# An FNet mixing and squared-ReLU FFN kernel: GpSimd's products get a second operation, and GpSimd squares one half of h in some steps

## The chip, the cores and the metric

One core of one Trainium2 chip runs the whole program. The metric is the device time of one execution in microseconds. The kernel before took a median of 609.28 us in three runs (609.07 to 609.3).

## The reference

What is computed is a two-dimensional Fourier mixing, of which the real part is kept, and a feed-forward layer with a squared ReLU behind it.

```python
X = np.fft.fft(x, axis=1)            # x: 8 x 3008 x 256
X = np.fft.fft(X, axis=2)
x = X.real.reshape(8 * 3008, 256)
h = np.maximum(x @ w_in, 0.0)        # w_in: 256 x 2048
out = h * h @ w_out                  # w_out: 2048 x 256
```

## The kernel before

**Symmetry.** The real part at token k is a cosine part minus a sine part, and at token S-k (S is 3008) the same two parts added. So the kernel works on token pairs. For each pair it keeps a cosine column (tile zc) and a sine column (tile zs), and from them it makes the hidden values of both tokens. The Fourier transform over the 256 model dimensions is folded into the input weights beforehand (tile gh, three sets: for zc, for zs, and minus two times the second).

**Blocks and steps.** The 12,040 pair columns are cut into 25 blocks (wins, numbered w = 0 to 24; most are 512 columns wide, some of the first 240 to 448, the last 360). A block has eight steps s = 0 to 7 (NST); a step makes 256 of the 2048 hidden rows for the block's tokens k and S-k. Results lie in the tile h2 as f16: for each of 16 row groups first the half for tokens k (here "the plus half", wn columns), then the half for S-k ("the minus half").

**A plain step** has these parts. pq (L832, L833): four matmuls on PE (TensorE) make the plus half in PSUM (tile ph). first, which is relu(s, 0) (L864): ACT (ScalarE) writes the ReLU of it to h2. others: sixteen or so matmuls of the second layer for the block before (L690), pieces of the folding of a later batch, and matmuls of the transform (L578). turn (L855): two more matmuls turn ph into the minus half. relu(s, 1) (L864): ACT writes its ReLU, reversed, to h2.

**A step with a product** (the steps in diff[w], from block 4 on) saves the two matmuls of turn. cosines (L841) makes the cosine part alone; twice (L845) has DVE (VectorE) form t = -2 ph + n; sines (L850) adds the sine part to ph; then ACT writes the plus half and DVE writes the minus half from t and ph (L862, a custom operation). The product n is a rank-one row for the Nyquist column: spread_nyq (L784, L785) spreads one row of zs over the partitions as zn, and nyq_rows (L793) has POOL (GpSimd) multiply zn, 128 x 512 f16, by one scalar per partition, twice for each such step, into f32. nyq gives them out in the last three steps of the block before. They have three buffers, so a product can wait for an older t.

**Which steps.** Blocks 4 and 5 have products in steps 4 and 6. Later blocks have them in steps 0, 2, 4 and 6, but blocks 8, 10, 13, 16 and 19 in 2, 4 and 6 and block 9 in 0 and 2. In blocks 4 to 24 this makes 73 steps with products and 95 plain steps.

**Squares.** keep puts a square on the list kept, and settle, called in the next step (behind pq in a plain step, behind twice in a step with a product), issues the list. In a plain step DVE squares both halves in place in one instruction of 2048 columns (power, L871). In step 7 the plus half is squared on its own at once and the minus half is kept. In a step with a product DVE squares the minus half and ACT the plus half (power_act, L875).

**Who uses h2.** The second layer of a block (ffn2_steps, L690) runs spread over the eight steps of the next block, 128 tokens of all 2048 hidden rows at a time: the plus half's tokens in the first half of that block, the minus half's in the second.

**Folding.** For each of the batches 2 to 7 DVE folds the input by its symmetries (two-input operations, L429, L433, L440, L443, L446, L458, later L486 and L497) in steps that put and late give, over three to four blocks. POOL's queue also issues the DMAs of it: the input (xo, L127 and L132), the way out to a scratch (scr, L462) and back (rb, L470, L472).

All engines run their instructions in the order in which they are written (manual_schedule).

Of the kernel before, what the change touches and what calls it, by code (L numbers as in the profile page):

```python
# [13 lines left out]
ALU = mybir.AluOpType  # L14
# [15 lines left out]
def kernel(  # L30
# [14 lines left out]
    nc = tc.nc  # L45
# [487 lines left out]
    g2n = const.tile([P, NFC], F32, name="g2n")  # L533
# [194 lines left out]
    NST = NFC // 2  # L728
    at_of = {w: [[] for _ in range(NST)] for w in range(NW)}
    post_of = {w: [[] for _ in range(NST)] for w in range(NW)}  # L730
    diff = {w: (0, 2, 4, 6) if w > 5 else (4, 6) for w in range(4, NW)}
# [37 lines left out]
    kept = []  # L769
    plus = []  # L770

    def settle():
        for k in kept:
            k()
        kept.clear()
        let_go()

    zns = {}
# [8 lines left out]
    def nyq_rows(wt, steps):  # L787
        wn1 = wins[wt][1]
        for s in steps:
            n2 = n2s[wt, s] = wp.tile([P, 2, WN], F32, name="n2", tag="w16")  # L790
            for a in range(2):
                fc = 2 * s + a
                nc.gpsimd.tensor_scalar(out=n2[:, a, 0:wn1], in0=zns[wt][:, 0:wn1], scalar1=g2n[:, fc : fc + 1], scalar2=None, op0=ALU.mult)  # L793

    old = None
    for w in range(NW):
        g0, wn = wins[w]
        h2 = h2p.tile([P, NFC, 2 * WN], F16, name="h2", tag="h2")
# [29 lines left out]
        def pq(s):  # L828
            ph = phs[s] = ps_h.tile([P, 2, 512], F32, name="ph", tag="psh")
            for a in range(2):  # L830
                f0 = (2 * s + a) * P
                nc.tensor.matmul(ph[:, a, 0:wn], gh[:, 0, f0 : f0 + P], zcw[:, 0:wn], start=True, stop=False)  # L832
                nc.tensor.matmul(ph[:, a, 0:wn], gh[:, 1, f0 : f0 + P], zsw[:, 0:wn], start=False, stop=True)  # L833
# [3 lines left out]
        def cosines(s):  # L837
            ph = phs[s] = ps_h.tile([P, 2, 512], F32, name="ph", tag="psh")
            for a in range(2):
                f0 = (2 * s + a) * P  # L840
                nc.tensor.matmul(ph[:, a, 0:wn], gh[:, 0, f0 : f0 + P], zcw[:, 0:wn], start=True, stop=True)  # L841

        def twice(s):
            t2 = t2s[s] = tmp.tile([P, 3 * NE], F32, name="t2", tag="tt")[:, 0 : 2 * WN].rearrange("p (a n) -> p a n", a=2)
            nc.vector.scalar_tensor_tensor(out=t2[:, :, 0:wn], in0=phs[s][:, :, 0:wn], scalar=-2.0, in1=n2s[w, s][:, :, 0:wn], op0=ALU.mult, op1=ALU.add)  # L845

        def sines(s):
            for a in range(2):
                f0 = (2 * s + a) * P
                nc.tensor.matmul(phs[s][:, a, 0:wn], gh[:, 1, f0 : f0 + P], zsw[:, 0:wn], start=False, stop=True, skip_group_check=True)  # L850

        def turn(s):
            for a in range(2):
                f0 = (2 * s + a) * P
                nc.tensor.matmul(phs[s][:, a, 0:wn], gh[:, 2, f0 : f0 + P], zsw[:, 0:wn], start=False, stop=True, skip_group_check=True)  # L855

        def relu(s, sg):
            h = h2[:, 2 * s : 2 * s + 2, sg * wn : (sg + 1) * wn]
            if sg:
                h = rev_dim(h, 2)  # L860
            if sg and s in t2s:
                nc.vector._custom_dve(TENSOR_ADD_SAT, out=h, in0=t2s[s][:, :, 0:wn], in1=phs[s][:, :, 0:wn], s0=BIG, s1=0.0)  # L862
            else:
                nc.scalar.activation(h, phs[s][:, :, 0:wn], AF.Relu, bias=0.0, scale=-1.0)  # L864

        def keep(*k):
            kept.append(lambda p=power: p(*k))

        def power(s, a, b, h2=h2, wn=wn):
            h = h2[:, 2 * s : 2 * s + 2, a * wn : b * wn]  # L870
            nc.vector.tensor_tensor(h, h, h, op=ALU.mult)  # L871
# [5 lines left out]
        def first(s):  # L877
            relu(s, 0)
            run(*plus)
            plus.clear()  # L880

        def others(s):
            for j in at[s]:
                j()
            for j in spread(f2, s, NST):
                j()
            for j in post[s]:
                j()
            if s == lo:
                zl[:] = [j for zu, part, h in zj for j in zu(part, h)]  # L890
            if s >= lo:
                for j in spread(zl, s - lo, hi - lo) if s < hi else []:
                    j()

        def nyq(s):
            if w + 1 in diff and hi < NST - 1:
                if s == hi:
                    spread_nyq(w + 1)
                    nyq_rows(w + 1, diff[w + 1][0:1])
                elif s == hi + 1:  # L900
                    nyq_rows(w + 1, diff[w + 1][1 : 2 if s < NST - 1 else None])
                elif s == hi + 2:
                    nyq_rows(w + 1, diff[w + 1][2:])
            if s == 0 and w in diff and w not in zns:
                spread_nyq(w)
                nyq_rows(w, diff[w])
# [33 lines left out]
        elif w == 1:  # L940
            zl = [j for zu, part, h in zj for j in zu(part, h)]
            for p in range(NST // 2):
                s0, s1 = 2 * p, 2 * p + 1
                f2q = spread(f2, p, NST // 2)
                n = len(f2q) // 4
                pq(s0)
                if p < 2:
                    settle()
                relu(s0, 0)
                pq(s1)  # L950
                relu(s1, 0)
                if s1 == NST - 1:
                    run(*post[s0 - 1])
                    settle()
                    power(s1, 0, 1)
                    run(*zl)
                run(*f2q[0:n])
                turn(s0)
                run(*f2q[n : 2 * n])
                turn(s1)  # L960
                relu(s0, 1)
                relu(s1, 1)
                run(*at[s0], *at[s1], *f2q[2 * n :])
                if p == 2:
                    settle()
                keep(s0, 0, 2)
                keep(s1, int(s1 == NST - 1), 2)
            gh_nyq()
        for s in range(NST) if w > 1 else ():
            held["on"] = s + 1 in diff.get(w, ()) or (s + 1 == NST and 0 in diff.get(w + 1, ()))  # L970
            if s in diff.get(w, ()):
                cosines(s)
                twice(s)
                settle()
                others(s)
                sines(s)
                first(s)
                relu(s, 1)
                keep(s, 1, 2)
                plus.append(lambda s=s, p=power_act: p(s))  # L980
                nyq(s)
                continue
            pq(s)
            settle()
            first(s)
            if s == NST - 1:
                power(s, 0, 1)
            others(s)
            nyq(s)
            turn(s)  # L990
            relu(s, 1)
            keep(s, int(s == NST - 1), 2)
        if 0 not in diff.get(w + 1, ()):
            held["on"] = False
            settle()
# [33 lines left out]
```

## Time and profile before

| | |
|---|---|
| median of three runs | 609.28 us |
| the profiled execution, whole | 609.91 us |
| its span, from the first to the last instruction | 608.1 us |
| PE busy | 589.3 us |
| DVE busy | 480.9 us |
| ACT busy | 463.7 us |
| POOL busy | 339.0 us, of which 265.3 products (L793) |
| squares on DVE (L871) | 194.1 us in 216 instructions |
| granted TensorE clock | 1.0 |

A group line of the profile reads: line, engine, operation, output tile <- input tiles, shapes and count, then busy time in us and the mean of one in ns, then the engine's idle time before them with what ended it. A line of the timeline reads: start in us, length in us, engine, line, operation, tiles, shapes, count, and in brackets the idle time before it. PEld is the loading of weights, which runs beside the matmuls.

### The profile page before, as it was taken

The numbers are of one execution on the slowest core, as the hardware profiler recorded it, in microseconds if no ns is written. First come the engines' busy times: TensorE is split into PE (matmuls) and PEld (weight loads), VectorE is DVE, ScalarE is ACT, GpSimd is POOL, SyncE is SP. The second block draws the span as 40 slices with busy tenths as digits, with TensorE's granted clock in tenths as the row PEclk, the third lists the DMA queues.
The fourth block names the chain that finished last, engine by engine and source line by source line (L and its number), as shares of the span: only waits on it lengthen the run. The fifth ranks groups of instructions, "written<-read, shape, count | busy, mean of one in ns | idle before, by whom it ended". The sixth has DMA issues, their size and how long they took to land.

```text
span 608.1 us, 11279 instructions
## 1 busy us (share of the span) xinstructions
PE 589.3 (97%) x4441; PEld 426.9 (70%) x4441; DVE 480.9 (79%) x591; ACT 463.7 (76%) x636; POOL 339.0 (56%) x248
## 2 busy tenths in 40 slices
PE   4899999999999999999999999999999999999997
PEld 2456777777677767777777777776777777777786
DVE  7787666977988968979889799787988788777760
ACT  6696778868787877787878787877787877778762
POOL 8312225179837555398374981858926756737610
PEclk9999999999999999999999999999999999999999
DMA  8846331126311271255112721136112211111112
GB/s 150 135 82 154 103 88 35 35 76 127 95 37 50 84 152 54 69 115 118 40 53 73 153 64 53 37 111 135 58 28 88 77 45 38 51 46 38 53 56 67
DMA packets 36524, 47.50 MB, mean 78 GB/s; under 512 B 4216, under 2 KB 30328, under 8 KB 36472
## 3 DMA queue, kind: packets, MB, share of 16 engines
q0 software_dynamic: 9344, 22.14, 18.0%
q1 hardware_dynamic: 26899, 24.44, 13.4%
q8 instruction: 34, 0.56, 0.4%
q10 hardware_dynamic: 228, 0.21, 0.1%
q14 instruction: 19, 0.15, 0.1%
HBM read 33.63 MB, written 27.84 MB: 101 GB/s over the span
## 4 chain that ended last, share of the span: by engine, by line
PE 78%; POOL 9%; DVE 6%; issue 3%; DMA 3%; ACT 1%; POOLq 0%; DVEq 0%
PE po L690 46%; PE ph L855 7%; PE ph L832 6%; PE ph L833 6%; PE ph L850 4%; PE ph L841 4%; POOL n L793 4%; PE pz L578 3%; DMA xo<-in_x_dram,idx_r 2%; POOL xo L132 1%; DVE h L871 1%; DMA scr<-ev 1%; DVE t L845 1%; POOL rb L472 1%; DVE h L862 1%
## 5 line engine op out<-in xcount | busy, mean ns | idle before, releaser
L690 PE MATMUL po<-wout,h 128*128 128x256 f16 (+1 forms) x3024 | 362.3, 273 | 0.0
L793 POOL TENSOR_SCALAR n<-zn,g2n 128x512 f32<-128x512 f16 (+2 forms) x146 | 265.3, 1832 | 167.6 <-ACT zn L785 167.2
L864 ACT ACTIVATE h<-ph 128x1024 f16<-128x1024 f32 (+3 forms) x311 | 295.5, 993 | 79.5 <-PE ph L850 60.1
L690 PEld LDWEIGHTS <-h 128*128 128x128 f16 (+1 forms) x3024 | 296.7, 98 | 72.1
L871 DVE TENSOR_TENSOR h<-h 128x1024 f16<-128x1024 f16 (+6 forms) x216 | 194.1, 909 | 33.2 <-ACT h L864 30.7
L862 DVE CUSTOM_DVE_ANT_0 h<-t,ph 128x1024 f16<-128x1024 f32 x67 | 81.6, 1218 | 34.4 <-ACT h L864 34.1
L845 DVE SCALAR_TENSOR_TENSOR t<-ph,n 128x1024 f32<-128x1024 f32 (+2 forms) x73 | 87.7, 1201 | 25.7 <-PE ph L841 22.4
L832 PE MATMUL ph<-zc,gh 128*128 128x512 f16 (+3 forms) x238 | 87.4, 368 | 0.4 <-ACT h L926 0.3
L833 PE MATMUL ph<-zs,gh 128*128 128x512 f16 (+3 forms) x238 | 87.4, 368 | 0.0
L875 ACT ACTIVATE h<-h 128x1024 f16<-128x1024 f16 (+2 forms) x73 | 76.5, 1048 | 0.0
L855 PE MATMUL ph<-zs,gh 128*128 128x512 f16 (+3 forms) x238 | 68.1, 368 | 0.2 <-ACT h L864 0.2
L705 ACT ACTIVATE osb<-po 128x512 f32<-128x512 f32 (+3 forms) x95 | 55.5, 589 | 10.6 <-PE po L690 10.0
L850 PE MATMUL ph<-zs,gh 128*128 128x512 f16 (+2 forms) x146 | 42.7, 374 | 1.9 <-DVE t L845 1.9
L841 PE MATMUL ph<-zc,gh 128*128 128x512 f16 (+2 forms) x146 | 42.8, 375 | 0.0
L833 PEld LDWEIGHTS <-gh 128*128 128x128 f16 x238 | 23.2, 98 | 25.7 <-issue 0.9
L832 PEld LDWEIGHTS <-gh 128*128 128x128 f16 x238 | 23.2, 98 | 25.0
L583 ACT ACTIVATE es<-pz 128x376 f32<-128x376 f32 (+1 forms) x32 | 14.9, 486 | 16.4 <-PE pz L578 16.3
L855 PEld LDWEIGHTS <-gh 128*128 128x128 f16 x238 | 22.3, 98 | 6.2 <-issue 0.3
L841 PEld LDWEIGHTS <-gh 128*128 128x128 f16 x146 | 14.3, 98 | 16.9 <-issue 0.5
L472 POOL DMA_INDIRECT rb<-scr,idx_r x16 | 20.2, 1261 | 4.9 <-issue 4.6
L132 POOL DMA_INDIRECT xo<-in_x_dram,idx_r x15 | 18.4, 1226 | 4.5 <-issue 4.3
L127 POOL DMA_DIRECT2D xo<-in_x_dram x8 | 6.4, 796 | 23.4 <-DVE fo L433 15.3
(143 smaller groups left out, 367.4 us busy)
## 6 DMA issues: line engine op xcount, KB each, us to landing
out_dram<-osb SPq DMA_DIRECT2D x77, 128.0 KB
xo<-in_x_dram POOLq DMA_DIRECT2D x7, 768.0 KB, 7.3
scr<-ev POOLq DMA_DIRECT2D x8, 390.0 KB, 3.7
rb<-scr POOLq DMA_DIRECT2D x16, 130.0 KB, 2.4
out_dram<-osb SPq DMA_DIRECT2D x12, 94.0 KB
w<-in_moe_w_in_dram POOLq DMA_DIRECT2D x2, 512.0 KB, 10.2
wout<-in_moe_w_out_dram POOLq DMA_DIRECT2D x1, 1024.0 KB, 15.7
out_dram<-osb SPq DMA_DIRECT2D x8, 75.0 KB
```

The costliest lines, as they stand in the source:

```text
L690: nc.tensor.matmul(po[0:m, j * D : (j + 1) * D], h2[:, fc, q : q + m], wout16[:, fc, :], start=(fc == 0), stop=(fc == NFC - 1))
L793: nc.gpsimd.tensor_scalar(out=n2[:, a, 0:wn1], in0=zns[wt][:, 0:wn1], scalar1=g2n[:, fc : fc + 1], scalar2=None, op0=ALU.mult)
L832: nc.tensor.matmul(ph[:, a, 0:wn], gh[:, 0, f0 : f0 + P], zcw[:, 0:wn], start=True, stop=False)
L833: nc.tensor.matmul(ph[:, a, 0:wn], gh[:, 1, f0 : f0 + P], zsw[:, 0:wn], start=False, stop=True)
L841: nc.tensor.matmul(ph[:, a, 0:wn], gh[:, 0, f0 : f0 + P], zcw[:, 0:wn], start=True, stop=True)
L845: nc.vector.scalar_tensor_tensor(out=t2[:, :, 0:wn], in0=phs[s][:, :, 0:wn], scalar=-2.0, in1=n2s[w, s][:, :, 0:wn], op0=ALU.mult, op1=ALU ...
L850: nc.tensor.matmul(phs[s][:, a, 0:wn], gh[:, 1, f0 : f0 + P], zsw[:, 0:wn], start=False, stop=True, skip_group_check=True)
L855: nc.tensor.matmul(phs[s][:, a, 0:wn], gh[:, 2, f0 : f0 + P], zsw[:, 0:wn], start=False, stop=True, skip_group_check=True)
L862: nc.vector._custom_dve(TENSOR_ADD_SAT, out=h, in0=t2s[s][:, :, 0:wn], in1=phs[s][:, :, 0:wn], s0=BIG, s1=0.0)
L864: nc.scalar.activation(h, phs[s][:, :, 0:wn], AF.Relu, bias=0.0, scale=-1.0)
L871: nc.vector.tensor_tensor(h, h, h, op=ALU.mult)
L875: nc.scalar.activation(h, h, AF.Square, bias=0.0, scale=1.0)
```

## The change

The products get a second operation, a multiplication by 1.0. In blocks that have steps with products (from block 4 on), a plain step's minus half is squared by POOL, in place, through the same list; DVE squares the plus half alone. Blocks 1 to 3 and the steps with products keep their squares as they are.

```diff
-nc.gpsimd.tensor_scalar(out=n2[:, a, 0:wn1], in0=zns[wt][:, 0:wn1], scalar1=g2n[:, fc : fc + 1], scalar2=None, op0=ALU.mult)
+nc.gpsimd.tensor_scalar(out=n2[:, a, 0:wn1], in0=zns[wt][:, 0:wn1], scalar1=g2n[:, fc : fc + 1], scalar2=1.0, op0=ALU.mult, op1=ALU.mult)
...
+        def keep_minus(s, h2=h2, wn=wn):
+            h = h2[:, 2 * s : 2 * s + 2, wn : 2 * wn]
+            kept.append(lambda: nc.gpsimd.tensor_tensor(h, h, h, op=ALU.mult))
...
             turn(s)
             relu(s, 1)
-            keep(s, int(s == NST - 1), 2)
+            if w in diff:
+                if s < NST - 1:
+                    keep(s, 0, 1)
+                keep_minus(s)
+            else:
+                keep(s, int(s == NST - 1), 2)
```

In POOL's queue the squares of a block stand between its products: in a block with products in 0, 2, 4, 6, those of steps 1 and 3, then two products for the next block, the square of step 5, six products, and the square of step 7.

## The prediction

> **What bounds the kernel now.** I read the page's table of engines first, then its groups of instructions, then the view of waits, and last stretches of the timeline.
>
> ```profile
> PE 589.3 (97%) x4441; PEld 426.9 (70%) x4441; DVE 480.9 (79%) x591; ACT 463.7 (76%) x636; POOL 339.0 (56%) x248
> ...
> L793 POOL TENSOR_SCALAR n<-zn,g2n 128x512 f32<-128x512 f16 (+2 forms) x146 | 265.3, 1832 | 167.6 <-ACT zn L785 167.2
> ...
> L871 DVE TENSOR_TENSOR h<-h 128x1024 f16<-128x1024 f16 (+6 forms) x216 | 194.1, 909 | 33.2 <-ACT h L864 30.7
> ```
>
> PE is busy for 97% of the span at a granted clock of 1.0, and its clock row shows 9 in all slices. Of the 18.8 us in which it is not busy, 6.4 lie before its first matmul and about 4 behind its last one.
>
> ```profile
> PE pw L327 <- DVE spn L321: 6.4, 1, 6.4
> ...
> DVE t L845 <- POOL n L793: 2.8, 2, 1.5
> ...
> PE ph L850 <- DVE t L845: 1.9, 4, 1.0
> ```
>
> The view of waits (engine and line, what it waited for, us, times, longest) says how little can be won: in blocks 4 to 24 PE waits for DVE's t (L845) 1.9 us in all, and part of that is DVE waiting for a product n of POOL (2.8 us in two waits). Counting the gaps between matmul starts there I find some 4 us. So DVE and POOL are not the bound, but PE has no cover against either: t must come between the cosines (L841) and the sines (L850).
>
> **What goes and comes on DVE.** The plan has 95 plain steps in blocks 4 to 24 (168 steps less 73 with a product). In most, DVE squared 2048 columns in 1.22 us (by form: 128x2048 mean 1259 ns) and now squares 1024 in 0.69; in the last step of a block one of two squares of 0.69 goes. That is some 0.53 us each, 50 us of DVE's 481. It lies beside PE and is worth only what it takes off the 4 us. Engines PE, ACT and SP keep their instructions.
>
> **What comes on POOL: 95 squares.** No large two-input operation of POOL is in this trace. Below: it must read 2048 elements. A product's read takes 0.44 us for 512 elements, 0.86 ns each (the added wait, below). With the 0.19 us that the smallest square-like row takes (L232, 128x2), 0.19 + 2048 x 0.86 = 1.94 us. Above: the product's whole rate and a second read. The shortest n of 512, 448 and 360 columns took 1.55, 1.40 and 1.18 us, so 0.28 us and 2.49 ns per element; 0.28 + 1024 x (2.49 + 0.86) = 3.7 us. I take 2.4, nearer to the lower end: the reads and a quarter of the distance to the upper end for what of the writing does not ride along.
>
> **What changes on POOL: 146 products with a second operation.** The trace has two-operation rows only for one or two columns; L219 took 0.30 us for one column, no more than the 0.28 us with which a one-operation n starts, so the start is not dearer. The rate is not shown. Below: IOTA writes 377 columns in 0.495 us and 128 in 0.282, 0.86 ns each, so 0.28 + 512 x 0.86 = 0.72 us. Above: one more pass at 0.86, 1.56 + 0.44 = 2.0 us. The unhindered n takes 1.56, of which the read is over after 0.55; the remaining 1.0 us for 512 writes is over twice IOTA's rate, so the one-operation form runs a path with waste in it, and the other form may run another path. I give "shorter" 0.7 and take 1.1, between 0.72 and 1.56.
> The Trainium skill (GPSIMD Engine Reference, section 3.1) gives 1.03 cycles per element for bodies of up to two operations, and about 2.5 for two inputs; the one-operation n contradicts the first (2.98 cycles at the page's 1.2 GHz). By the page a product would take an estimated 0.72 us and a square 2.4.
>
> **Does it fit?** The stretch 381.1 to 454.1 us is one batch (blocks 16, 17, 18).
>
> ```profile
> core 0: us, PE busy (x) PEld busy (x) DVE busy (x) ACT busy (x) POOL busy (x), PEclk, DMA share, GB/s
> 381.10:405.70 24.60, 24.60 (x195) 17.97 (x194) 20.45 (x23) 19.78 (x29) 17.00 (x11) 1.00 0.18 57
> 405.70:431.10 25.40, 24.85 (x183) 17.67 (x181) 20.07 (x26) 19.41 (x28) 21.87 (x16) 1.00 0.55 124
> 431.10:454.10 23.00, 23.00 (x170) 16.53 (x169) 21.75 (x24) 17.90 (x24) 10.65 (x8) 1.00 0.15 43
> ```
>
> POOL is busy 49.5 of 73.0 us, with 22 products of mean 1.83 and the DMA issues. 13 squares add 31.2 and products of 1.1 take off 22 x 0.73 = 16: 64.7 of 73.0. It fits, at 89%. With products as now it is 80.7: 7.7 us too much per batch. The squares' own deadline is loose: PE reads that half from step 4 of the next block, some 12 us later. The DMA issues behind a square (scr, rb, xo) come 2 to 5 us later; rb is used five steps (15 us) on, xo over a block on, so they cost nothing while POOL fits.
>
> **The wait that is added: POOL and DVE exclude each other.**
>
> ```profile
> 12.47 1.76 DVE L399 TENSOR_TENSOR u<-xo 128x3072 f16<-128x3072 f16 x1
> ...
> 12.61 1.71 POOL L225 TENSOR_SCALAR evs<-evec 128x2 f32<-128x2 f32 x1
> ...
> 343.63 4.83 POOL L793 TENSOR_SCALAR n<-zn,g2n 128x512 f32<-128x512 f16 x3
> ...
> 345.32 1.11 DVE L871 TENSOR_TENSOR h<-h 128x1024 f16<-128x1024 f16 x1
> ```
>
> A POOL operation on two columns lasts 1.71 us because it ends 0.09 us behind DVE's two-input operation at 14.23. The other way round, the second n of the group at 343.63 starts at 345.20; DVE's square begins 0.13 us later and takes 1.11 instead of 0.69: it stands until 0.55 us after the n's start. Squares begun 0.37 and 0.47 us into an n lose 0.18 and 0.08; those begun after 0.55 nothing. So POOL holds what both need for its reads alone, 0.44 us for an n. L845 and L862, with one input in PSUM, are not touched. A square reads four times as much: 1.75 us of hold, at 0.86 ns per element.
> The Trainium skill (SBUF — State Buffer, "Who interferes with whom") calls this an exclusive lock for the whole instruction. The trace agrees on the exclusion but shows the hold of an n ending at a third of it. By "whole instruction" a hold of 2.4 would put 0.65 us on each collision below, 30 x 0.65 = 20 us on the sum.
>
> Now one pair of steps, plain then with product:
>
> ```profile
> 515.10 1.03 ACT L864 ACTIVATE h<-ph 128x1024 f16<-128x1024 f32 x1
> ...
> 515.40 1.22 DVE L845 SCALAR_TENSOR_TENSOR t<-ph,n 128x1024 f32<-128x1024 f32 x1 [0.54 <-PE ph L841]
> 516.54 1.22 DVE L871 TENSOR_TENSOR h<-h 128x2048 f16<-128x2048 f16 x1
> ...
> 518.57 1.22 DVE L862 CUSTOM_DVE_ANT_0 h<-t,ph 128x1024 f16<-128x1024 f32 x1 [0.81 <-ACT h L864]
> ```
>
> The half that goes to POOL is ready when ACT ends at 516.13. POOL, if free, takes the hold at about 516.2 to 518.0. DVE's own square, free at 516.54, stands 1.4 us and is over at 518.7 instead of 517.76: 0.9 us later though it is half as long. L862 follows with 0.81 us of slack: 0.1 lost, and PE has some 0.7 us before it needs that PSUM buffer back. So a bare pair costs nothing. Where a fold operation (0.96 us, L429 to L458, L486) stands behind the square, DVE has no slack, the 0.9 to 1.0 us stays, and beyond PE's 0.7 some 0.3 us of PE stall is left. Per batch I count about five such steps in the order of put and late, 30 in six batches: +9 us. Against it stand the stalls that go with shorter products and less DVE work, about 3 of the 4 us. Sum +6. The last block's squares have 720 columns, and PE first does three groups of the other half (5.5 us): nothing.
>
> **The number.** The profiled execution took 609.9 us (span 608.1, 1.8 around it); +6 is 616. The median shown is 609.28, 0.6 below it: **615**.
>
> **Rivals.**
> - *POOL becomes the bound.* Products as now, or squares above 3 us. Then every t waits for its n and PE for t: 7.7 us per batch, six batches, +46: 655. Ends: square 1.94 with the product as now, 49.5 + 25.2 - 73.0 = 1.7 per batch, 620; square 3.7 with it, 24.6 per batch, 758. It decides from 49.5 + 13 squares + 22 changes of the product over 73. For it: the only measured large product is 1.56. Chance 0.25. In it the second operation doesn't shorten anything.
> - *Faster: DVE's relief wins.* If POOL gives up its hold between pieces of its read, or gets to its square after DVE's own, no DVE operation stands over 0.55 us, and 0.53 us less per plain step removes the late t's; a short n removes the waits on n. At most the 4 us, likely 2 to 3: 606.5. It decides below a stand of 0.53 us per square. For it: an n holds only 0.44. Chance 0.25.
> - *No difference*: stalls come and go alike, 608 to 610.5. Chance 0.12.
> - *The forecast*, short products and DVE standing behind squares, 611 to 625: 0.38.
>
> A measurement of this kernel can tell about 0.2% (1.2 us) from nothing. Slower 0.38 + 0.25 = 0.63, same 0.12, faster 0.25. Range: 604 (all of the 4 us and a little) to 655, which leaves out the longer half of the POOL case and a few per cent below.
>
> **What would show it.** Right: n at about 0.7 to 1.2 us; squares on POOL of 2 to 3 us; DVE's 128x1024 squares in plain steps over 1.5 us where they begin inside a POOL square; PE's waits for DVE t (L845) rising from 1.9 us to around 10, in fold blocks. Wrong: n still at 1.56 and POOL over 90% busy, with DVE t waiting for POOL n by tens of us (then 655); or DVE's squares all at 0.69 and no wait of PE left (then 606).

## The result

The changed kernel takes a median of 659.25 us (655.27 to 659.75, four runs) against 609.17 us for the kernel before: a ratio of 1.0801, 95% interval 1.0776 to 1.0826. It is slower by some 50 us (49.1 us between the spans of the two profiled executions). The forecast was slower, at 615 with a range up to 655; the time lies outside that range.

The page of the changed kernel, engines and the groups that answer to those shown before (the product is still L793, the square of DVE is now L875, that of POOL L871):

```profile
PE 601.8 (92%) x4441; PEld 429.0 (65%) x4441; DVE 529.7 (81%) x570; ACT 465.5 (71%) x636; POOL 389.2 (59%) x343
...
L871 POOL TENSOR_TENSOR h<-h 128x1024 f16<-128x1024 f16 (+2 forms) x95 | 188.3, 1992 | 93.3 <-ACT h L864 92.2
L875 DVE TENSOR_TENSOR h<-h 128x1024 f16<-128x1024 f16 (+5 forms) x195 | 216.6, 1123 | 18.6 <-ACT h L864 16.0
L793 POOL TENSOR_SCALAR n<-zn,g2n 128x512 f32<-128x512 f16 (+2 forms) x146 | 132.5, 921 | 94.5 <-ACT zn L785 91.8
```

The products fell from 1832 to 921 ns on average (unhindered, with no DVE operation in the way, 0.69 us; 1.56 before). POOL got 95 squares of 2.0 us and is still only 59% busy, so POOL is not full. DVE was to lose 50 us of work and is busy 49 us more: L875 does less than L871 did before and takes 216.6 us instead of 194.1, and folding operations became longer too. The view of waits, PE's rows:

```profile
PE ph L850 <- DVE t L845: 27.3, 13, 4.6
PE ph L841 <- DVE h L862: 9.3, 14, 1.8
```

These were 1.9 us and nothing. PE now waits for DVE, and DVE's own records are long because it stands in them. PE's idle time grew from 18.8 to 55.4 us and its busy time by 12.5 us.

Part of the busy time is the granted clock, 0.985 in the profiled execution (1.0 before). The trace shows where it fell: to one half for 3.4 us, five times between the start-up and the last matmul, in blocks 6, 10, 11, 14 and 17. Each of these stretches begins within 1 us of the end of one of PE's five waits of over 2 us (2.2 to 4.6 us). Behind the other 22 waits of the two rows above, of up to 1.8 us, it did not fall. The wait of block 17 and three windows around it:

```profile
463.42 0.86 PE L850 MATMUL ph<-zs,gh 128*128 128x512 f16 x2 [4.28 <-DVE t L845]
```

```profile
core 0: us, PE busy (x) PEld busy (x) DVE busy (x) ACT busy (x) POOL busy (x), PEclk, DMA share, GB/s
459.20:463.50 4.30, 0.08 (x1) 0.08 (x1) 4.30 (x4) 0.53 (x2) 1.87 (x2) 1.00 0.21 62
463.60:467.00 3.40, 3.40 (x12) 1.61 (x11) 3.00 (x7) 2.00 (x3) 0.00 (x0) 0.50 0.02 8
467.00:471.00 4.00, 4.00 (x34) 3.06 (x32) 2.44 (x4) 2.99 (x5) 1.48 (x3) 1.00 0.11 36
```

At half the clock 3.4 us do the work of 1.7, so the five stretches come to an estimated 8.5 us of the 49.

**The hold, measured.** I added up, over the two-input operations of DVE from 94 us on, how much longer each lasts than the same shape alone; this is called the stand below. It is 7.5 us before and 105.8 us after, in 92 operations. (The squares of 896 and 720 columns, in the blocks of 448 and 360, are not in these sums; with them it is some 111 us after.) Where a POOL square runs alone and at its own pace (1.89 us), DVE gets through 1.75 us after that square's start, in every such case. A bare pair of steps, DVE's rows and POOL's:

```profile
581.93 1.22 DVE L845 SCALAR_TENSOR_TENSOR t<-ph,n 128x1024 f32<-128x1024 f32 x1 [0.33 <-PE ph L841]
583.08 1.90 DVE L875 TENSOR_TENSOR h<-h 128x1024 f16<-128x1024 f16 x1
585.46 1.22 DVE L862 CUSTOM_DVE_ANT_0 h<-t,ph 128x1024 f16<-128x1024 f32 x1 [0.49 <-ACT h L864]
```

```profile
582.53 1.89 POOL L871 TENSOR_TENSOR h<-h 128x1024 f16<-128x1024 f16 x1 [1.48 <-ACT h L864]
```

The square of DVE should take 0.69 us; it starts 0.55 us into POOL's and takes 1.90. L862 behind it still waits for ACT, so nothing is lost here, as the forecast had it for a bare pair. Now POOL's queue and DVE's around the first half of block 17 (443.6 to 475.0 us):

```profile
442.46 1.13 POOL L470 DMA_DIRECT2D rb<-scr  x2
443.90 1.36 POOL L472 DMA_INDIRECT rb<-scr,idx_r  x1 [0.30 <-issue]
445.56 0.97 POOL L472 DMA_INDIRECT rb<-scr,idx_r  x1 [0.31 <-issue]
446.56 1.37 POOL L793 TENSOR_SCALAR n<-zn,g2n 128x512 f32<-128x512 f16 x2
448.10 1.02 POOL L132 DMA_INDIRECT xo<-in_x_dram,idx_f  x1 [0.16 <-issue]
449.10 0.62 POOL L127 DMA_DIRECT2D xo<-in_x_dram  x1
450.03 1.01 POOL L132 DMA_INDIRECT xo<-in_x_dram,idx_r  x1 [0.30 <-issue]
451.35 0.94 POOL L132 DMA_INDIRECT xo<-in_x_dram,idx_r  x1 [0.31 <-issue]
452.33 3.18 POOL L793 TENSOR_SCALAR n<-zn,g2n 128x512 f32<-128x512 f16 x4
455.48 5.59 POOL L871 TENSOR_TENSOR h<-h 128x1024 f16<-128x1024 f16 x3
```

```profile
455.48 6.15 DVE L875 TENSOR_TENSOR h<-h 128x1024 f16<-128x1024 f16 x1
461.55 0.69 DVE L486 TENSOR_TENSOR xy<-rb 128x1040 f16<-128x1040 f16 x1
462.16 1.21 DVE L845 SCALAR_TENSOR_TENSOR t<-ph,n 128x1024 f32<-128x1024 f32 x1
```

From 442.5 to 452.3 POOL issues the DMAs of a load and of the way back and two products, then four products; meanwhile three squares (step 7 of block 16, steps 1 and 3 of block 17) pile up behind them. They run in one row, and DVE's square stands for all three: 6.15 us for 0.69 us of work. The next t is late, and PE with it: that is the wait of 4.28 us shown above.

A folding operation can stand by itself too. Here the third square of a row follows DVE's own square, and L443 takes 2.66 us instead of 0.96:

```profile
504.25 6.04 POOL L871 TENSOR_TENSOR h<-h 128x1024 f16<-128x1024 f16 x3
```

```profile
506.82 1.72 DVE L875 TENSOR_TENSOR h<-h 128x1024 f16<-128x1024 f16 x1
508.46 2.66 DVE L443 TENSOR_TENSOR ab<-fo 128x1560 f16<-128x1560 f16 x1
```

The lengths of blocks (from the first matmul of step 0 to that of the next block) say where the time came from, in us:

| blocks | before | after |
|---|---|---|
| 22, 23 (no folding) | 23.99, 22.76 | 23.99, 22.76 |
| 12, 15, 18, 21 | 22.82 to 23.02 | 23.52 to 24.03 |
| 8, 13, 16, 19 (folding) | 23.75 to 24.54 | 27.15 to 27.55 |
| 10 (folding, two batches close together) | 24.47 | 30.21 |
| 6, 11, 14, 17 (behind a load) | 24.44 to 25.45 | 30.32 to 31.39 |
| 9, 20 | 25.60, 24.73 | 26.20, 25.65 |
| 4, 5, 7 | 22.16 to 24.16 | 23.47 to 25.15 |

A long stand is not always dear: DVE stands 3.2 us in block 9 (at 231.9 us) and 2.9 us in block 20 (at 534.3 us), and these blocks lose only 0.6 and 0.9 us.

### The profile page after: what moved, and what is told of

Read it like the earlier page. It is cut to its first block, busy times and chain, and to the rows that moved or that the text cites. A ratio compares the mean times of both kernels' runs of the same rounds, so it can differ in the third digit from the quotient of the medians.

```text
span 657.2 us, 11347 instructions
## 1 busy us (share of the span) xinstructions
PE 601.8 (92%) x4441; PEld 429.0 (65%) x4441; DVE 529.7 (81%) x570; ACT 465.5 (71%) x636; POOL 389.2 (59%) x343
## 3 DMA queue, kind: packets, MB, share of 16 engines
q1 hardware_dynamic: 26899, 24.44, 12.5%
## 4 chain that ended last, share of the span: by engine, by line
PE 63%; DVE 25%; issue 5%; ACT 2%; POOL 2%; DMA 1%; DVEq 0%; ACTq 0%; POOLq 0%
PE po L690 35%; DVE h L875 8%; DVE t L845 6%; PE ph L832 5%; PE ph L855 5%; PE ph L833 5%; PE ph L841 4%; PE ph L850 4%; DVE h L862 3%; PE pz L578 3%; DVE ab L443 2%; DVE xy L497 2%; DMA xo<-in_x_dram,idx_r 1%; DVE fe L429 1%; ACT h L864 1%
## 5 line engine op out<-in xcount | busy, mean ns | idle before, releaser
L690 PE MATMUL po<-wout,h 128*128 128x256 f16 (+1 forms) x3024 | 366.6, 275 | 0.3 <-DVE h L875 0.3
L871 POOL TENSOR_TENSOR h<-h 128x1024 f16<-128x1024 f16 (+2 forms) x95 | 188.3, 1992 | 93.3 <-ACT h L864 92.2
L875 DVE TENSOR_TENSOR h<-h 128x1024 f16<-128x1024 f16 (+5 forms) x195 | 216.6, 1123 | 18.6 <-ACT h L864 16.0
L793 POOL TENSOR_SCALAR n<-zn,g2n 128x512 f32<-128x512 f16 (+2 forms) x146 | 132.5, 921 | 94.5 <-ACT zn L785 91.8
L862 DVE CUSTOM_DVE_ANT_0 h<-t,ph 128x1024 f16<-128x1024 f32 x67 | 81.4, 1215 | 43.8 <-ACT h L864 43.6
L832 PE MATMUL ph<-zc,gh 128*128 128x512 f16 (+3 forms) x238 | 89.5, 377 | 0.9 <-DVE h L862 0.4
L833 PE MATMUL ph<-zs,gh 128*128 128x512 f16 (+3 forms) x238 | 89.7, 377 | 0.0
L850 PE MATMUL ph<-zs,gh 128*128 128x512 f16 (+2 forms) x146 | 43.6, 381 | 27.8 <-DVE t L845 27.3
L855 PE MATMUL ph<-zs,gh 128*128 128x512 f16 (+3 forms) x238 | 68.1, 368 | 0.2 <-ACT h L864 0.2
L833 PEld LDWEIGHTS <-gh 128*128 128x128 f16 x238 | 23.6, 99 | 27.8 <-issue 4.3
L832 PEld LDWEIGHTS <-gh 128*128 128x128 f16 x238 | 23.4, 98 | 25.7 <-issue 1.1
L850 PEld LDWEIGHTS <-gh 128*128 128x128 f16 x146 | 13.5, 97 | 33.2 <-issue 30.5
L841 PEld LDWEIGHTS <-gh 128*128 128x128 f16 x146 | 14.2, 97 | 28.5 <-issue 13.5
L855 PEld LDWEIGHTS <-gh 128*128 128x128 f16 x238 | 22.2, 97 | 6.0 <-issue 0.5
L472 POOL DMA_INDIRECT rb<-scr,idx_r x16 | 18.4, 1151 | 4.9 <-issue 4.9
```

The source lines that it names most:

```text
L690: nc.tensor.matmul(po[0:m, j * D : (j + 1) * D], h2[:, fc, q : q + m], wout16[:, fc, :], start=(fc == 0), stop=(fc == NFC - 1))
L871: kept.append(lambda: nc.gpsimd.tensor_tensor(h, h, h, op=ALU.mult))
```

## Experiments

**Theory.** DVE stands behind POOL's reads of SBUF, and the time is lost where the stand meets folding work or is several squares long. **Rivals**: POOL's queue is what is late (full, or its squares too late for PE); the clock fell for a reason of its own; or every square simply costs its share.

**e1_products**: the second operation alone, squares as before.

```diff
-... scalar2=None, op0=ALU.mult)
+... scalar2=1.0, op0=ALU.mult, op1=ALU.mult)
```

> One part alone: the products have their second operation, all squares stay on DVE as before. Theory (DVE stands behind POOL's squares, 106 us of stands in the changed kernel, and gives back more than the 50 us it was relieved of): none of the 50 us is here; n at 0.69 us, DVE's waits for n gone (2.8 us before), 606 to 608.5 us. Rival (POOL's queue is what is late): the same, so this run parts the two halves of the change and not the theories. If the time is above 611, the second operation itself harms.

Measured: 609.42 us, ratio 0.9996 (0.9986 to 1.0007). POOL's products take 144.4 us instead of 265.3 and the time doesn't change. The loss of 50 us comes only with the squares on POOL.

The even time is a balance. Blocks 6, 8 and 17 are 1.2, 0.3 and 0.7 us shorter, blocks 15, 18 and 20 are 0.5 to 0.6 us and blocks 12 and 21 0.2 us longer. Short products in a row can make DVE stand as well; this square takes 3.78 us behind five of them:

```profile
479.12 3.78 DVE L871 TENSOR_TENSOR h<-h 128x1024 f16<-128x1024 f16 x1
```

Block 20, in which it lies, is one of those 0.5 us longer.

**e2_squares**: the squares alone, products with one operation. The edit is the other hunks of the change without that line.

> The other part alone: POOL squares the minus half in plain steps, the products keep one operation. Theory (stands): DVE's stands of about 106 us stay, and POOL, with 49.5 + 13 x 2.0 = 75 us of work per 73 us, is now full too, so its squares stand in longer rows: 660 to 700 us. Rival (queue): POOL's work alone is what counts, per batch 75 against 49.5 - 22 x 0.9 + 26 = 56 in the changed kernel, so this must be slower than the changed kernel by over 30 us, with DVE waiting for n.

Measured: 682.46 us, ratio 1.1183 (1.1139 to 1.1228), clock 0.963. The waits show what comes on top when POOL is late as well:

```profile
DVE t L845 <- POOL n L793: 24.2, 13, 2.9
PE po L690 <- POOL h L871: 24.2, 5, 6.4
```

Products late for t, and now squares late for the second layer. Stands are 74.6 us, fewer than in the changed kernel, perhaps because DVE waits elsewhere first; my "about 106" missed that. The time is in the range of the theory and 23 us above the changed kernel, where the rival asked for over 30 with DVE waiting for n, which it does; so this run alone does not part them. The second operation is thus worth 23 us to a kernel with the squares on POOL, and nothing without them.

**e4_left_out**: the minus half of plain steps is squared by nobody.

```diff
-            kept.append(lambda: nc.gpsimd.tensor_tensor(h, h, h, op=ALU.mult))
+            pass
```

> As the changed kernel, but the minus half of plain steps is squared by nobody (left out). It is the most that taking these squares from DVE could bring. Theory (stands): 604 to 607.5 us, as the fill or a little below it. Rival (the clock granted to PE fell for a reason of its own): the clock stays at 0.98 to 0.99 and the time above 612 us.

Measured: 608.76 us, ratio 0.9979 (0.9966 to 0.9992), clock 1.0. Had POOL's squares cost nothing at all, the change could have brought 0.2%, about 1.3 us (0.5 to 2.1 by the interval). The rival falls: without the squares the clock is back. The time is a little above what I expected: I had taken most of the 4 us of PE's gaps to be DVE's.

**e5_fill**: POOL as long occupied, but only writing (the minus half stays unsquared). Three fills of 720 columns stand for one of 2200 (e3_fill, planned first), which had no room in SBUF, so e3_fill gave no time.

```diff
+    fill = const.tile([P, 720], F16, name="fill")
...
-            kept.append(lambda: nc.gpsimd.tensor_tensor(h, h, h, op=ALU.mult))
+            kept.append(lambda: (nc.gpsimd.memset(h[:, :, 0:1], 0.5), nc.gpsimd.memset(fill, 0.5), nc.gpsimd.memset(fill, 0.5), nc.gpsimd.memset(fill, 0.5)))
```

> As the changed kernel, but where POOL squared the minus half of a plain step it waits for the same ACT result, sets one column of it and then fills a tile of 720 columns, which nobody reads, three times: about as long as a square (1.9 us), without reading SBUF. The minus half of plain steps stays unsquared. Theory (DVE stands because POOL reads SBUF): stands under 15 us in all, as where the squares are left out, and 607 to 611 us. Rival (POOL's occupation, the lateness of its queue or its writing is what counts): near 659 us.

Measured: 609.3 us, ratio 0.9992 (0.9979 to 1.0004), clock 0.998, stands 9.8 us. The page's POOL groups:

```profile
L872 POOL MEMSET fill<- 128x720 f16 x285 | 198.5, 697 | 11.4
L794 POOL TENSOR_SCALAR n<-zn,g2n 128x512 f32<-128x512 f16 (+2 forms) x146 | 125.9, 876 | 50.3 <-ACT zn L786 49.8
```

198.5 us of filling stand where 188.3 us of squares stood, in the same queue, and 50 us are gone. So POOL's occupation and the lateness of its queue are not the cause. What the fill leaves out is the reading (and the writing over all of h, which e6 keeps without a loss). The clock is back at 0.998, as it should be if the half-speed stretches come from PE's long waits.

**e6_one_input**: the same place, one input of 1024 columns instead of two (the half stays unsquared).

```diff
-            kept.append(lambda: nc.gpsimd.tensor_tensor(h, h, h, op=ALU.mult))
+            kept.append(lambda: nc.gpsimd.tensor_scalar(out=h, in0=h, scalar1=1.0, scalar2=1.0, op0=ALU.mult, op1=ALU.mult))
```

> As the changed kernel, but POOL multiplies the minus half of a plain step by 1.0 twice in place (one input of 1024 columns) instead of squaring it (two inputs): the half stays unsquared. A dose between square and fill. Theory (the hold is the read): about 1.1 us each, a hold of 0.14 + 1024 x 0.86 = 1.0 us instead of 1.75, stands of 40 to 60 us instead of 106, 615 to 635 us. Rival (it is two inputs on POOL that exclude DVE, not any read): no stands beyond 15 us, 607 to 611 us.

Measured: 609.84 us, ratio 0.9997 (0.9984 to 1.001). Stands are 40.1 us in 86 operations, as the theory has it, so an operation of POOL with one input excludes DVE's two-input operations too. But they cost nothing, where I expected 6 to 25 us. Nearly all are 0.84 us or shorter (two are 0.90 and 1.46). PE's row shows it:

```profile
PE ph L850 <- DVE t L845: 1.1, 3, 0.4
```

The sum of the stands doesn't set the cost. Single stands of up to 0.84 us are covered by the order of this kernel, folding or not; what a longer one costs depends on where it falls (block 9 above, and block 20 in e1).

**e7_own_first**: DVE squares its plus half in the same step, so that POOL's square no longer gets ahead of it.

```diff
-            if s == NST - 1:
+            if s == NST - 1 or w in diff:
                 power(s, 0, 1)
...
             if w in diff:
-                if s < NST - 1:
-                    keep(s, 0, 1)
                 keep_minus(s)
```

> As the changed kernel, but DVE squares its plus half in the same step, right behind ACT's ReLU of it, and not at the next step's list, where POOL's square of the minus half begins 0.4 us ahead of it. Theory A (what costs is that POOL gets ahead of DVE's own square each time): the stands of those squares, 74 of 106 us, go; the ones of the folding stay, 32 us: 615 to 630 us. Theory B (what costs is rows of POOL squares and the folding's two-input operations behind them): those squares are not what costs, and DVE's wait for ACT is new: 640 to 665 us.

Measured: 663.36 us, ratio 1.0895 (1.0826 to 1.0964). The stands of DVE's squares fell from 74.0 to 37.9 us, those of L429 to L497 grew from 32 to 42, and PE waits 34.8 us for t. So 36 us less of those stands saved nothing, and theory A, with its 615 to 630 us, falls. The meeting alone is not priced by this run: in the new order DVE also waits longer for ACT (for L862 and L875 114.5 us in all, 63.5 in the changed kernel).

**e8_no_rows**: the 15 squares that pile up behind a load go back to DVE.

```diff
+    folded_at = (5, 8, 10, 13, 16)
+    rows = {(v, 7) for v in folded_at} | {(v + 1, q) for v in folded_at for q in (1, 3)}
...
-            if w in diff:
+            if w in diff and (w, s) not in rows:
```

> As the changed kernel, but the 15 squares that pile up behind the DMA issues of a load (step 7 of the blocks 5, 8, 10, 13, 16, and steps 1 and 3 of the block behind each) are DVE's again. In the changed kernel POOL makes three of them in a row and DVE stands 3 to 5.5 us at a time. Theory B (rows): the blocks 6, 11, 14 and 17 lose their extra 5.6 to 6.4 us each and block 9 nothing, some 22 us in all: 633 to 640 us. Theory A (each square costs its share): 15 of 95 squares, 8 us: 649 to 653 us.

Measured: 635.88 us, ratio 1.0416 (1.0384 to 1.0449), clock 0.997. Blocks 11, 14 and 17 take 25.44 us, block 6 23.85; they had 30.3 to 31.4. PE's rows (lines are 2 higher in this kernel):

```profile
PE ph L852 <- DVE t L847: 12.5, 10, 2.2
PE ph L843 <- DVE h L864: 9.4, 14, 1.8
```

Its wait for t fell from 27.3 us in 13, the longest 4.6, to 12.5 with a longest of 2.2. 15 squares of 95 made 23 of 50 us, where an even share is 8: theory A, the rival of even shares, falls. PE's busy time fell by 6.5 us with them (601.8 to 595.3): from block 4 on no half-speed stretch is left. The run takes the squares away; it does not spread the same squares out, so that the row itself is what costs is read from the trace at 455.48 us and from the places where the time came back.

**e9_no_folds**: in addition the squares of the folding blocks 8, 10, 13, 16 and 19 go back (the edit is shown against e8_no_rows).

```diff
-    rows = {(v, 7) for v in folded_at} | {(v + 1, q) for v in folded_at for q in (1, 3)}
+    rows = {(v, 7) for v in folded_at} | {(v + 1, q) for v in folded_at for q in (1, 3)} | {(v, q) for v in (8, 10, 13, 16, 19) for q in range(8)}
```

> As e8_no_rows, and the squares of the blocks 8, 10, 13, 16 and 19, in which DVE makes most of a batch's folding, are DVE's again as well (GpSimd keeps 55 of 95). In e8 these five blocks take 3.0 to 4.2 us longer than before, 16.7 us in all, with folding operations (L443, L458) standing 1.7 us behind a square. Theory (a stand costs only where the folding leaves DVE no room; the 0.84 us stands of e6 cost nothing, the 1.7 us ones do): these blocks come back to before, 618 to 622 us. Rival (each square costs its share of the 27 us that e8 still loses, 80 squares): 25 squares, 8.4 us, 626 to 629 us.

Measured: 622.37 us, ratio 1.0206 (1.0191 to 1.0221), clock 1.0. Blocks 13, 16 and 19 fall from 27.55 to 24.98 us; 24.54 was before. This is just beyond the end of what the theory gave and clear of the rival. My counts were off: step 7 of blocks 8, 10, 13 and 16 had gone back in e8 already, so 21 squares and not 25 went back here, and POOL keeps 59 and not 55. By shares that would be some 7 us; it was 13.5.

**e10_bare**: POOL squares only in the blocks 7 and 21 to 24.

```diff
-            if w in diff:
+            if w in (7, 21, 22, 23, 24):
```

> As the changed kernel, but GpSimd squares only in the blocks 7, 21, 22, 23 and 24, where next to nothing is folded (20 of 95 squares). Theory (bare pairs have cover): blocks 22 to 24 as before, blocks 7 and 21 up to 1 us longer: 609 to 611 us, no gain, as the squares left out altogether were worth only 0.2%. Rival (each square costs its share of the 50 us): 20 squares, 10.5 us, 620 us.

Measured: 611.61 us, ratio 1.0043 (1.0029 to 1.0057). Blocks 22 to 24 are as before, block 7 takes 25.03 instead of 24.16 and block 8 24.56 instead of 23.75. A little more than I said and far from 620. No version with POOL's squares beat the kernel before, and e4 says why there is almost nothing to win.

## Why the prediction was wrong

- **What bounds the kernel: right.** Relief of DVE is worth 0.2% (e4), a short product nothing by itself (e1). I gave "about 3 of the 4 us"; it is near 1.
- **Products: shorter, as said, and by more.** I took 1.1 us; unhindered they take 0.69, just under my lower end of 0.72 (0.92 on average). From the 1.03 cycles per element of the Trainium skill (GPSIMD Engine Reference, section 3.1) I had estimated 0.72, and the two-operation form agrees with it; the one-operation form does not.
- **Squares: too dear, harmlessly.** I took 2.4 us with a lower end of 1.94; alone they take 1.89. The two-input floor of the Trainium skill (GPSIMD Engine Reference, section 2.1, and not 3.1 as the prediction has it) with its 2.5 cycles, from which 2.4 was estimated as well, is not borne out: 128x720 takes 1.39 us and 128x1024 1.89, so 1.65 ns per element, an estimated 2.0 cycles at the page's 1.2 GHz. POOL fits, as said, and the rival in which POOL becomes the bound did not happen; that its 655 lies close to the measured time is chance. In e2, where the products are long, it happens in part: DVE waits 24.2 us for n.
- **The hold: right within 0.1 us.** 1.75 us of hold was worked out, beginning some 0.1 us behind a square's start, so DVE should get through after 1.85 us or so; it does after 1.75. That the digits agree is luck. The Trainium skill (SBUF — State Buffer, "Who interferes with whom") calls it the whole instruction. For the square that is nearly so (1.75 of 1.89), for the one-operation product it was 0.55 of 1.56; in e5 memsets, which only write, left 9.8 us of stands.
- **The bare pair: right.** Blocks 22 and 23 are unchanged to 0.01 us.
- **The step that failed** is the size of one term: "some 0.3 us of PE stall is left. Per batch I count about five such steps ..., 30 in six batches: +9 us". The runs put 50 us there. The count was near: PE's waits for DVE's t and h, shown above, are 27, against 1.9 us in 4 before. The size was not: they last 1.4 us on average (36.6 us in all), and the half-speed stretches behind the longest, which the sum does not have, add an estimated 8.5 us. Two things were missing. First, rows: I asked what the DMA issues lose behind the squares ("they cost nothing while POOL fits") and not what the squares do behind the DMA issues. They wait for them, come out three at a time, and DVE stands up to 5.5 us: 23 us (changed kernel to e8). Second, I let only DVE's square stand, while a folding operation behind it can stand 1.7 us on its own in the same pair; the folding blocks lost 13.5 us (e8 to e9). The remaining 59 squares cost 12.7 us, thinly spread (e9 to before; of it some 2 us in the 20 squares of e10); what each single one meets was not taken apart. Together that is 49.6 us, taken off in this order, the lower clock included.
- **The cover: not contradicted.** I gave PE 0.7 us before a late DVE is felt; stands of 0.84 us cost nothing in e6.

**Open.** In the row at 455.48 us DVE did not get in between POOL's squares; at 507.9 us, between a second and a third, it did. What decides this wasn't tried. The granted clock fell behind PE's long waits (0.985, and 0.963 in e2), but not behind each: in e7 PE waits 3.1 us in blocks 11 and 14, and the clock stays at 1.0 behind them. What decides that is open too.

## What to carry to other kernels

Before work moves to an engine that can shut a busy one out, find the longest single time for which the busy one can be shut out, not the sum: look at what stands ahead of the moved work in its queue, since work that waits there comes out in a row. Compare that time with the slack in front of the next instruction that the bounding engine waits for. And price the relief first, by leaving the work out altogether: here it was worth 0.2%.

## What the runs showed of the hardware

- A multiplication by a scalar per partition on GpSimd, 128x512 f16 to f32, takes 1.56 us with one operation and 0.69 us with a second one, times 1.0 (unhindered; means 1832 and 921 ns).
- A two-input product of 128x1024 f16 on GpSimd takes 1.89 us, and keeps two-input operations of VectorE out for 1.75 us; several in a row can keep them out from the first to the last (three: 5.46 us). Two-operation products in a row can do it too (five in e1: 3.1 us). In e5, with memsets as long, 9.8 us of such stands are left of 105.8.
- In the changed kernel the granted TensorE clock was 0.50 for 3.4 us behind each of PE's five waits of 2.2 to 4.6 us, and behind none of the 22 of up to 1.8 us.
